# A transformer block in fp32: first MLP weights split during the attention and kept in DRAM

## The chip, the cores and the metric

The kernel runs on one core of a Trainium2 chip. The metric is device time in microseconds (us) of one execution. PE is TensorE, PEld its weight loads, DVE is VectorE, ACT is ScalarE, POOL is GpSimd, and SP is SyncE, which here issues every DMA.

## The reference

One block on 2048 tokens of width 576, fp32, with 32 query heads that share one key and value head of 18 columns:

```python
mod = (silu(c) @ w_mod).reshape(1, 6, 1, 576)
sa, ca, ga, sb, cb, gb = (mod[:, i] for i in range(6))
h = layernorm(x) * (1 + ca) + sa
q = h @ wq                       # 32 heads of 18
k, v = h @ wk, h @ wv            # one head
p = softmax(q k^T * 18 ** -0.5)  # 2048 x 2048 per head
x = x + ga * ((p v) @ wo)
h = layernorm(x) * (1 + cb) + sb
y = layernorm(h)
x = x + gb * (gelu(y @ w1 + b1) @ w2 + b2)   # hidden width 4608
```

## The kernel before

All matrix products on PE use fp32r operands. A value is kept as a high part, which is the value rounded to fp32r, and a low part, which is the value less the high part; a product is then three products (high-high, high-low, low-high). Making such a pair costs a copy and a subtraction, and where these are made is a large share of what ACT, DVE and POOL do.

The order of the work is written out by hand. Every engine runs its instructions in the order in which the program states them, and so does SP with its DMAs: an instruction that waits holds back all that stand behind it on its engine.

**Stage 1** makes the projections and the first layer norm. **Stage 2** is the attention. It goes through 32 "quads" (n = 0 to 31: four blocks of 512 tokens, by eight groups of four heads). A quad has 16 slots (kc = 0 to 15, 128 keys each). In a slot PE makes scores (`st_mm`, L792), ACT takes their exponentials (L794), and PE multiplies by V (`pv_mm`, L781); beside that PE makes the scores again in the other orientation for the NEXT quad (L313, L802), and DVE takes the row maxima (L814, L812). At the end of each slot `between(n, kc)` adds the rest:

- At kc = 12 and 13 (`smax_fin1`, `smax_fin2`) the maxima of the next quad are put together, transposed, split by POOL into `ms` (L355, L356) and sent by four DMAs into the query tile `qst` of the next quad (L360).
- `post_quad` normalizes the finished quad, one piece a slot: DVE transposes (L616), POOL multiplies by the reciprocal into `T` (L620), DVE transposes back (L622), ACT and POOL split it (L629, L630), and four DMAs put `os` into the attention's result (L634).
- At kc = 1 `load_q` clears and loads a query tile (two POOL memsets, L130; six DMAs, L309).
- In odd slots the queue `fill` takes one step. It holds the `wo` product of a finished block (L593, eight steps) and then, for blocks 0 and 1, the MLP's norm (`ln2_block`, four `ln2_tile` of 128 tokens each).
- In odd slots from n = 3 on, the queue `prep` takes one step. Before the change it makes the split pairs of the second MLP weights: load, scale by BC (L715), copy (L718), subtract (L720), write to the DRAM tensor `w2scr` (L721).

`ln2_tile` is two layer norms in a row on one tile. POOL does the multiplications by BC and the addition of `b2` always; the two passes that subtract the mean and scale (L534, L548) run on POOL where `fine` is true, for blocks 0 and 1, and on DVE for blocks 2 and 3, which are done inside the MLP. PE then transposes the tile in two steps.

**Stage 3** starts with the `wo` product of the last block (tiles t = 0 to 3, two halves each) and then runs the MLP in 36 rounds (v = 0 to 35): 18 groups g of 256 hidden columns, for the first 1024 tokens and again for the last. A round makes seven products with a Strassen-like scheme (`product`, L944): operands A11, S2, S3, A12, S1, A22, S4 of the first weights, the S ones being sums or differences of blocks. It then runs the GELU (L956 to L964) and, one round later, the second product (`fc2`, L979), whose result DVE adds to `XT` (L983). Before the change the seven operands of round v + 1 are made anew inside round v: `load_w1` loads the raw weights (L657), `w1_sum`, `w1_part` and `w1_tails` form sums and pairs on POOL (L664, L667, L683, L702 to L706) and ACT (L662). `first_split` does this for round 0 in the last quad. `load_w2` reads the pairs of the second weights from `w2scr`. `op_pieces` forms the other side's operands from the transposed norm, in rounds 0 and 17. The norm tiles of blocks 2 and 3 are taken step by step by `more` in rounds 1 to 16; a step that ends in "T" marks a PE transpose, which only some places take.

The pool `px`, which holds the working tiles of `prep` and `post_quad`, has one buffer for each name, unless a tile says otherwise:

```python
    pxp = tc.tile_pool(name="px", bufs=1, reuse_waits="tile")
```

Of the kernel before, what the change touches and what calls it, by code (L numbers as in the profile page):

```python
# [15 lines left out]
NB = 4  # L16
TB = S // NB
NT = TB // 128
KD = 5
# [13 lines left out]
def block_kernel(ctx: ExitStack, tc, x, wqkv, wo, w1, b1, w2, b2, c, wmod, ident_in, out):  # L33
# [31 lines left out]

    w2scr = dr.tile([NG, 128, 2, 2, D], F32, name="w2scr")
# [429 lines left out]
    def late_weights():  # L496

        gab = pb.tile([128, D], F32, name="gab")
        for j, dst, scl in ((2, gab, 1.0), (5, BC[:, 2, :], 0.5)):
            wm = load_mod(j)  # L500
            for _ in range(4):
                yield
            yield from mod_bcast(wm, px.tile([128, 640], F32, name="Z2"), dst, 0.0, scl)
        wor = bigw(D)
        sy.dma_start(wor, wo)
        wos = pw.tile([128, 2, KD, D], F32R, name="wos", tag="wA", padded_shape=[128, 2, KD, WQC])
        WOH, WOL = WO["h"], WO["l"] = wos[:, 0], wos[:, 1]
        for k in range(KD + 2):
            if k < KD:
                po.tensor_mul(wor[:, k, :], wor[:, k, :], gab)  # L510
            if 0 <= k - 1 < KD:
                ac.activation(WOH[:, k - 1, :], wor[:, k - 1, :], AF.Copy)
            if k >= 2:
                po.tensor_tensor(WOL[:, k - 2, :], wor[:, k - 2, :], WOH[:, k - 2, :].bitcast(F32), op=ALU.subtract)
            yield

    def ln2_tile(tb, t):
# [6 lines left out]
        fine = tb < 2  # L524
# [31 lines left out]
        yield None if fine else "T"  # L556
# [50 lines left out]
    def post_quad(n, PV):  # L607
# [13 lines left out]
        yield  # L621
        ve.transpose(O, T.rearrange("p a b -> p (a b)"))  # L622
# [18 lines left out]
    W1 = {}  # L641

    def w1_tile():
        W1["r"] = per.tile([128, 40, 128], F32R, name="w1a", tag="big", bufs=3)

    def w1_rooms():
        while prep:
            step(prep)
        W1["a"] = px.tile([128, KD, 2, 128], F32, name="w1r")
        t = px.tile([128, 3, 128], F32, name="w1s")  # L650
        W1["s"], W1["d"] = t[:, :2], t[:, 2]

    def w1_raw(f, h):
        return W1["a"][:, 2 * h:2 * h + 2, f, :]

    def load_w1(i):
        sy.dma_start(W1["a"].rearrange("p k f c -> p k (f c)"), w1[i])  # L657

    def w1_hi(a, n, src, e=ac):
        o = W1["r"][:, a:a + n]  # L660
        if e is ac:
            ac.activation(o, src, AF.Copy)  # L662
        else:
            e.tensor_copy(o, src)  # L664

    def w1_lo(a, n, src, e):
        e.tensor_tensor(W1["r"][:, 17 + a:17 + a + n], src, W1["r"][:, a:a + n].bitcast(F32), op=ALU.subtract)  # L667

    def w1_part(a, lo, e=po):

        n, src = (4, W1["a"][:, :KD - 1, 0, :]) if a == 0 else (2, w1_raw(1, 1))
        if lo:
            w1_lo(a, n, src, e)
        else:
            w1_hi(a, n, src)

    SUMS = {4: "S2", 6: "S3", 10: "S1", 12: "S4"}

    def w1_sum(a, e=po):

        o = W1["s"]
        def op(x, y, how):
            e.tensor_tensor(o, x, y, op=how)  # L683
        if SUMS[a] == "S3":
            op(w1_raw(0, 0), w1_raw(1, 0), ALU.subtract)
        elif SUMS[a] == "S4":
            op(w1_raw(0, 1), W1["r"][:, 4:6].bitcast(F32), ALU.subtract)
            op(o, W1["r"][:, 21:23].bitcast(F32), ALU.subtract)
        else:
            op(w1_raw(1, 0), w1_raw(1, 1), ALU.add)  # L690
            if SUMS[a] == "S2":
                op(o, w1_raw(0, 0), ALU.subtract)
        w1_hi(a, 2, o, e if e is po else ac)
        w1_lo(a, 2, o, e)

    def w1_tails(lo, e=po):

        t, d = W1["a"][:, KD - 1], W1["d"]
        if not lo:
            w1_hi(14, 2, t)  # L700
            return
        e.tensor_tensor(d, t[:, 0], t[:, 1], op=ALU.subtract)  # L702
        e.tensor_copy(W1["r"][:, 16], d)
        for o, i in ((slice(14, 16), t), (16, d)):
            h = W1["r"][64:, o]
            e.tensor_tensor(h, i[64:], h.bitcast(F32), op=ALU.subtract)  # L706

    def w2_parts():

        for g in range(NG):  # L710
            for f in range(2):
                o = px.tile([128, D], F32, name="w2o", tag="w1s")
                sy.dma_start(o, w2[g, :, f, :])
                yield
                po.tensor_tensor(o, o, BC[:, 2, :], op=ALU.mult)  # L715
                yield
                hl = px.tile([128, 2, D], F32R, name="w2p", tag="w1r")
                po.tensor_copy(hl[:, 0], o)  # L718
                yield
                po.tensor_tensor(hl[:, 1], o, hl[:, 0].bitcast(F32), op=ALU.subtract)  # L720
                sy.dma_start(w2scr[g, :, :, f, :], hl.bitcast(F32))  # L721
                yield

    prep = deque([w2_parts()])

    def first_split():
        w1_tile()
        w1_rooms()
        load_w1(0)
        for _ in range(3):  # L730
            yield
        w1_sum(4, ve)
        w1_part(0, False)
        yield
        w1_part(0, True)
        w1_sum(6, ve)
        yield
        w1_part(8, False)
        w1_sum(10, ve)
        w1_tails(False)  # L740
        yield
        w1_part(8, True)
        w1_sum(12, ve)
        yield
        w1_tails(True)
        yield
# [69 lines left out]
    def between(n, kc):  # L816
# [10 lines left out]
        if kc == 0 and n == NQT - 1:  # L827
            fill.append(first_split())
# [4 lines left out]
        if kc % 2:  # L833
            step(fill)
            if n > 2:
                step(prep)

# [34 lines left out]
    def op_pieces(R, e2):  # L872
# [23 lines left out]
    wop = {(t, h2): (psC if t == 3 and h2 else psM if t < 2 and t + h2 < 2 else psB)()  # L896
           for t in range(NT) for h2 in range(2)}
    for t in range(NT):
        for h2 in range(2):
            wo_mm(NB - 1, t, h2, wop[t, h2], 0, KD - 1)  # L900
# [8 lines left out]
    pwp.__exit__(None, None, None)  # L909
    px = ctx.enter_context(tc.tile_pool(name="mx", bufs=1, reuse_waits="tile"))  # L910
    tl = ctx.enter_context(tc.tile_pool(name="tl", bufs=1, side="right", reuse_waits="tile"))
    TL.append(tl.tile([128, 4, TB], F32R, name="opt"))
    form("+t0 -t0")
    for t in range(NT):
        for h2 in range(2):
            wo_mm(NB - 1, t, h2, wop[t, h2], KD - 1, KD)
            wo_add(NB - 1, t, h2, wop[t, h2])
    form("+t1 =T4 =T1 +T1 -t1 -T1")
    open_ps("3", 4)
    w1_rooms()  # L920
    B2["b"] = load_b2()
    load_w1(1)
    GT = big()
    U = px.tile([128, 2, TB], F32, name="u")
    W2 = [px.tile([128, 2, D], F32R, name="w2s", bufs=3) for _ in range(3)]
    W2.append(W1["r"][:, 31:40].rearrange("p a b -> p (a b)").rearrange("p (f c) -> p f c", f=2))
    W2 = W2[:2], W2[2:]
# [6 lines left out]
    def product(o, w, b, first=True, tail=None):  # L934

        h, l = W1["r"][:, w:w + 2], W1["r"][:, 17 + w:19 + w]
# [3 lines left out]
        if tail:  # L940
            wt = W1["r"][:, 14 + tail[0]]
            terms += [(wt, TL[0][:, tail[1]]), (wt, TL[0][:, 2 + tail[1]])]
# [6 lines left out]
    def gelu(v, f, b, p):  # L949
# [13 lines left out]
        ac.activation(GT[:, 2 * u], h, AF.Copy)  # L963
        po.tensor_tensor(GT[:, 2 * u + 1], h, GT[:, 2 * u].bitcast(F32), op=ALU.subtract)  # L964

    def fc2(v):
        h2, l2 = W2[v % 2]
        for bt in range(2 * NT):
# [3 lines left out]
            for nn in range(2):  # L972
                cs = slice(288 * nn, 288 * (nn + 1))
                terms = []
                for f in range(2):
                    gh, gl = (GT[:, 2 * G[v, b, f] + l, ts_] for l in range(2))
# [27 lines left out]
    for v in range(NV):  # L1004
        nx = v + 1 < NV
# [5 lines left out]
        def more(half="", first="", room=False):  # L1011

            if v in (0, NG - 1, NG):
                form(first if v == 0 else half if v == NG - 1 else "-T1 -B22 -t1" if first == "+T4" else "")
# [5 lines left out]
        def wt(f, *a):  # L1020
            if nx:
                f(*a)

        load_w2(v)
        ba = psB()
        product(ba, 0, 0)
# [4 lines left out]
        product(bb, 4, 6)  # L1031
# [6 lines left out]
        product(bc, 6, 10)  # L1038
        ve.tensor_tensor(U[:, 1], bc, U[:, 0], op=ALU.add)
        wt(w1_sum, 4)  # L1040
        more("-T2 =T3", "+B22", True)
        t_()
        if v == 1:
            t_()
        product(ba, 2, 2, False, (0, 0))
        gens.append(gelu(v, 0, 0, ba))
        g_()
        wt(w1_part, 0, False)
        more("+T3 +B21", "-B22", True)
        t_()  # L1050
        g_()
        wt(w1_sum, 6)
        wt(w1_part, 0, True)
        bd = psB()
        product(bd, 10, 8, True, (1, 1))
# [5 lines left out]
        more("-T3 -B21 =T4")  # L1061
        t_()
        g_()
        wt(w1_sum, 10)
        product(bc, 8, 12, False, (1, 0))
# [4 lines left out]
        wt(w1_part, 8, False)  # L1070
        more("=T1 +T4 +t0")
# [3 lines left out]
        wt(w1_part, 8, True)  # L1075
        product(bd, 12, 4, False, (2, 1))
# [4 lines left out]
        wt(w1_tails, False)  # L1081
        t_()
        wt(w1_sum, 12)
        wt(w1_tails, True)
        more("-T4 -t0 +T1 +B22 +t1")
        drain(f2)
        f2 = fc2(v)
        if v + 2 < NV:
            load_w1((v + 2) % NG)
# [43 lines left out]
```

## Time and profile before

| | |
|---|---|
| median of 3 runs | 2371.99 us (2367.28 to 2372.89) |
| the profiled execution | 2367.2 us, its span 2365.4 us |
| granted PE clock | 0.993 |
| busy | PE 2310.6, DVE 1822.6, ACT 1693.2, POOL 1157.7 us |
| DMA | 155.30 MB, 66 GB/s on average |

The profile shows one execution. Rows of a group give busy time, the mean of one instruction in ns, and the idle time of the engine before them with what ended it. "x <- y" in a row of waits means that x waited for y. "SPq" is SP's queue, and its durations are the issue of the DMA, not the transfer. The attention lasts from about 139 us to 1433 us, the MLP from there to the end; a quad is some 38 to 51 us, a round some 24 to 32.

### The profile page before, as it was taken

What the parts mean: (1) busy time and instruction counts of PE and PEld (TensorE: products, weight loads), DVE (VectorE), ACT (ScalarE), POOL (GpSimd) and SP (SyncE); (2) the same over time, 40 slices, a digit from 0 to 9 for tenths busy, and PEclk for the clock granted to TensorE, in tenths of its full rate; (3) what the DMA queues carried; (4) which work ended last, traced back from release to release, by engine and by line L of the source; (5) the groups of instructions that cost most, each with busy time, mean ns of one, the idle gap of its engine ahead of it and who ended that gap; (6) DMA issues with size and microseconds to landing.
All of it is one profiled execution on the core that took longest, in us unless ns stands there. A gap on an engine that the chain in (4) does not pass through costs nothing.

```text
span 2365.4 us, 44038 instructions
## 1 busy us (share of the span) xinstructions
PE 2310.6 (98%) x16586; PEld 1456.1 (62%) x16586; DVE 1822.6 (77%) x3242; ACT 1693.2 (72%) x3264; POOL 1157.7 (49%) x1402
## 2 busy tenths in 40 slices
PE   8999999999999999999999999999999999999999
PEld 5643444454344443444544436889898989999998
DVE  6589999979999889999799955666676665565655
ACT  5569999979999889999799996444444544444443
POOL 6501332324552235431101013888888787777774
PEclk9999999999999999999999999999999999999999
DMA  6412122211222112200000001211211221212112
GB/s 219 141 60 72 39 67 64 75 55 50 66 68 78 45 54 70 62 19 22 9 19 22 19 23 37 94 63 63 94 63 63 94 103 63 94 63 93 64 69 86
DMA packets 63206, 155.30 MB, mean 66 GB/s; under 512 B 7835, under 2 KB 11547, under 8 KB 62993
## 3 DMA queue, kind: packets, MB, share of 16 engines
q1 hardware_dynamic: 62993, 152.48, 19.5%
q8 instruction: 131, 2.15, 0.4%
q14 instruction: 82, 0.67, 0.1%
HBM read 108.17 MB, written 35.39 MB: 61 GB/s over the span
## 4 chain that ended last, share of the span: by engine, by line
PE 89%; DVE 3%; ACT 3%; POOL 3%; issue 1%; DMA 1%; SPq 0%; POOLq 0%; DVEq 0%; ACTq 0%
PE psC L781 21%; PE psA L979 19%; PE psB L944 17%; PE psB L792 11%; PE psM L313 10%; PE psB L802 4%; PE psB L593 2%; PE psB L242 2%; ACT P L794 2%; DVE mx L814 1%; PE psB L150 1%; PE psA L313 1%; PE psB L197 1%; ACT O L612 1%; DMA bigw<-in_wmod 0%
## 5 line engine op out<-in xcount | busy, mean ns | idle before, releaser
L794 ACT ACTIVATE P<-psB 128x512 f32<-128x512 f32 x2048 | 1051.4, 623 | 5.1 <-PE psB L792 3.9
L814 DVE TENSOR_REDUCE mx<-psM 128x1 f32<-128x512 f32 x1476 | 944.3, 683 | 57.5 <-PE psM L313 33.0
L781 PE MATMUL psC<-P,V 128*32 128x256 f32 (+1 forms) x6056 | 599.5, 467 | 13.1 <-ACT O L612 13.1
L313 PE MATMUL psM<-KS,qst 64*128 64x512 f32 x1722 | 595.8, 432 | 5.0 <-DVE mx L814 5.0
L792 PE MATMUL psB<-qst,KS 64*128 64x512 f32 x2048 | 600.0, 435 | 0.3 <-DMA qst<-ms 0.3
L979 PE MATMUL psA<-w2s,big 128*128 128x288 f32 x2880 | 498.1, 297 | 8.5 <-DVE XT L983 8.5
L979 PEld LDWEIGHTS psA<-w2s,big 128*128 128x128 f32 x2880 | 434.6, 190 | 23.7 <-DVE XT L983 9.7
L792 PEld LDWEIGHTS psB<-qst,KS 64*128 64x128 f32 x2048 | 306.2, 185 | 166.9 <-issue 72.5
L944 PE MATMUL psB<-ops,w1a 128*128 128x512 f32 x1512 | 390.8, 398 | 4.6 <-POOL w1a L667 2.1
L313 PEld LDWEIGHTS psM<-KS,qst 64*128 64x128 f32 x1722 | 285.1, 185 | 125.5 <-DVE mx L812 84.4
L983 DVE TENSOR_TENSOR XT<-psA,XT 128x576 f32<-128x576 f32 x288 | 216.7, 753 | 180.0 <-PE psA L979 179.7
L944 PEld LDWEIGHTS psB<-ops,w1a 128*128 128x128 f32 x1512 | 273.7, 189 | 56.0 <-POOL w1a L667 2.6
L781 PEld LDWEIGHTS psC<-P,V 128*32 128x32 f32 x6056 | 119.7, 108 | 232.8 <-issue 209.1
L963 ACT ACTIVATE big<-gx 128x512 fp32r<-128x512 f32 x144 | 91.1, 633 | 234.8 <-DVE gx L962 234.8
L964 POOL TENSOR_TENSOR big<-gx,big 128x512 fp32r<-128x512 f32 x144 | 187.3, 1301 | 129.6 <-ACT big L963 89.6
L805 ACT ACTIVATE xc<-psB 128x512 f32<-128x512 f32 x246 | 148.1, 602 | 91.4 <-PE psM L313 76.1
L355 POOL CAST ms<-mf 16x128 fp32r<-16x128 f32 x32 | 9.0, 280 | 408.8 <-ACT mf L354 408.8
L956 ACT ACTIVATE gx<-psB,b1t 128x512 f32<-128x512 f32 x144 | 97.3, 675 | 105.8 <-PE psB L944 97.3
L979 PE MATMUL psA<-w1a,big 128*128 128x288 f32 x576 | 169.7, 295 | 0.0
L812 DVE CUSTOM_DVE_ANT_0 xc<-psM,xc 128x512 f32<-128x512 f32 x246 | 167.4, 680 | 0.0
L960 ACT ACTIVATE psB<-gs 128x512 f32<-128x512 f32 x144 | 86.5, 601 | 94.3 <-DVE gs L959 94.3
L959 DVE SCALAR_TENSOR_TENSOR gs<-psB,gx 128x512 f32<-128x512 f32 x144 | 98.8, 686 | 70.2 <-ACT psB L957 70.1
(168 smaller groups left out, 2626.2 us busy)
## 6 DMA issues: line engine op xcount, KB each, us to landing
w2s<-w2scr SPq DMA_DIRECT2D x54, 576.0 KB
w1r<-in_w SPq DMA_DIRECT2D x36, 640.0 KB
w2scr<-w2p SPq DMA_DIRECT2D x36, 576.0 KB
qst<-qscr SPq DMA_DIRECT2D x192, 72.0 KB
w2o<-in_w SPq DMA_DIRECT2D x36, 288.0 KB
w1a<-w2scr SPq DMA_DIRECT2D x18, 576.0 KB
qscr<-qs SPq DMA_DIRECT2D x16, 504.0 KB
big<-os SPq DMA_DIRECT2D x112, 72.0 KB
```

The source lines that it names most:

```text
L313: pe.matmul(o, QST[n][64 * g:64 * g + 64, p, 128 * qt:128 * (qt + 1)], KS[64 * g:64 * g + 64, 512 * kb:512 * (kb + 1)], start=True, stop=True)
L781: pe.matmul(PVt[n][32 * j:32 * (j + 1), cs], V[:, kc, :], t[:, j, cs], start=(kc == 0 and h0 == 0), stop=(kc == 15), skip_group_check=True)
L792: pe.matmul(t, KS[64 * g:64 * g + 64, 128 * kc:128 * (kc + 1)], QST[n][64 * g:64 * g + 64, i, :], start=True, stop=True)
L794: ac.activation(P[n, kc][:, 2 * i + g, :], t, AF.Exp, scale=SCALE)
L805: ac.activation(XC[-1], t, AF.Relu)
L812: ve.tensor_tensor_reduce(c, t, c, 1.0, -3.0e38, ALU.add, ALU.max, o)
L814: ve.tensor_reduce(o, t, axis=AX.X, op=ALU.max)
L944: pe.matmul(o, x, y, start=(first and i == 0), stop=(i == len(terms) - 1), skip_group_check=True)
L959: ve.scalar_tensor_tensor(s, p, 1.0 / GA3, h, op0=ALU.add, op1=ALU.mult)
L964: po.tensor_tensor(GT[:, 2 * u + 1], h, GT[:, 2 * u].bitcast(F32), op=ALU.subtract)
L979: pe.matmul(p[:, nn, :288], x, y, start=(q == 0), stop=(q == len(terms) - 1))
L983: ve.tensor_tensor(Xv, p[:, :, :288], Xv, op=ALU.add)
```

## The change

The seven operands of each group of first weights, as split pairs, are made once, in the attention, by POOL, and written to a new DRAM tensor `w1scr` (18 groups of 128 x 31 x 128). The generator `weight_parts` takes the place of `w2_parts` in the queue `prep` and makes both weights of a group in 15 steps. `prep` is stepped in every slot from n = 3 on except slots 10 to 13, in place of odd slots alone. In the MLP each operand is loaded from `w1scr` in place, right after the product that read the one before it; the code that made them there goes, and so does `first_split`. `ln2_tile` is `fine` for all blocks. In `post_quad` there is one more slot between POOL's T and DVE's transpose. The last block's `wo` product uses the MLP's PSUM layout: three tiles ahead of it, the fourth in pieces within round 0.

```diff
+    w1scr = dr.tile([NG, 128, 31, 128], F32, name="w1scr")
...
-        gab = pb.tile([128, D], F32, name="gab")
+        gab = px.tile([128, D], F32, name="gab", tag="r2")
...
-        fine = tb < 2
+        fine = True
...
-        yield None if fine else "T"
+        yield "T"
...
         e.tensor_tensor(T, T, R[:, :, None].to_broadcast([128, 16, 32]), op=ALU.mult)
         yield
+        if e is po:
+            yield
         ve.transpose(O, T.rearrange("p a b -> p (a b)"))
...
+    OPS = ("A11", "S2", "A12", "S3", "S1", "A22", "S4")
+    def load_w1(i, what):
+        for w in what.split():
+            a = 4 * OPS.index(w) if w in OPS else 28
+            b = min(a + 4, 31)
+            sy.dma_start(W1["r"][:, a:b].bitcast(F32), w1scr[i, :, a:b])
+
+    def weight_parts():
+        def two(o, n, src, lo=None):
+            po.tensor_copy(o[:, :n], src)
+            po.tensor_tensor(o[:, n:2 * n], src, o[:, :n].bitcast(F32), op=ALU.subtract)
         for g in range(NG):
+            raw = px.tile([128, KD - 1, 2, 128], F32, name="r1")
+            sy.dma_start(raw.rearrange("p k f c -> p k (f c)"), w1[g][:, :KD - 1])
+            yield
+            yield
+            def blk(f, h):
+                return raw[:, 2 * h:2 * h + 2, f, :]
+            def part(w, src):
+                o = px.tile([128, 4, 128], F32R, name="r2")
+                two(o, 2, src)
+                a = 4 * OPS.index(w)
+                sy.dma_start(w1scr[g, :, a:a + 4], o.bitcast(F32))
+            sm = px.tile([128, 2, 128], F32, name="r3")
+            def add(x, y, how=ALU.subtract):
+                po.tensor_tensor(sm, x, y, op=how)
+            part("A11", blk(0, 0))
+            yield
+            part("A12", blk(0, 1))
+            yield
+            part("A22", blk(1, 1))
+            add(blk(1, 0), blk(1, 1), ALU.add)
+            yield
+            part("S1", sm)
+            add(sm, blk(0, 0))
+            yield
+            part("S2", sm)
+            add(blk(0, 1), sm)
+            yield
+            part("S4", sm)
+            add(blk(0, 0), blk(1, 0))
+            yield
+            part("S3", sm)
+            raw = px.tile([128, 2, 128], F32, name="r1")
+            sy.dma_start(raw.rearrange("p f c -> p (f c)"), w1[g][:, KD - 1])
+            yield
+            yield
+            d = px.tile([128, 128], F32, name="r3")
+            o = px.tile([128, 3, 128], F32R, name="r2")
+            po.tensor_tensor(d, raw[:, 0], raw[:, 1], op=ALU.subtract)
+            for x, y in ((o[:, :2], raw), (o[:, 2], d)):
+                po.tensor_copy(x, y)
+                po.tensor_tensor(x[64:], y[64:], x[64:].bitcast(F32), op=ALU.subtract)
+            sy.dma_start(w1scr[g, :, 28:31], o.bitcast(F32))
+            raw = px.tile([128, 2, D], F32, name="r1")
+            sy.dma_start(raw, w2[g])
+            yield
+            yield
+            po.tensor_tensor(raw, raw, BC[:, 2:3, :].to_broadcast([128, 2, D]), op=ALU.mult)
+            yield
             for f in range(2):
+                for nn in range(2):
+                    cs = slice(288 * nn, 288 * (nn + 1))
+                    o = px.tile([128, 2, 288], F32R, name="r2")
+                    two(o, 1, raw[:, f:f + 1, cs])
+                    sy.dma_start(w2scr[g, :, :, f, cs], o.bitcast(F32))
                 yield
+    prep = deque([weight_parts()])
...
-        if kc == 0 and n == NQT - 1:
-            fill.append(first_split())
...
             step(fill)
-            if n > 2:
+        if n > 2 and (kc < 10 or kc > 13):
+            step(prep)
+        if kc == 8 and n == NQT - 1:
+            while prep:
                 step(prep)
+            W1["r"] = per.tile([128, 40, 128], F32R, name="w1a", tag="big", bufs=3)
+            load_w1(0, " ".join(OPS) + " tails")
...
-                    ve.tensor_tensor(o, x, y, op=ALU.subtract)
+                    (e2 if w == "=T1" else ve).tensor_tensor(o, x, y, op=ALU.subtract)
...
+    open_ps("3", 4)
+    wop = {}
+    def wo_tile(t, k0, k1):
+        if t not in wop:
+            p = psA() if t != 2 else None
+            wop[t] = [psB()[:, :288] if t == 2 else p[:, h2, :288] for h2 in range(2)], p
         for h2 in range(2):
+            wo_mm(NB - 1, t, h2, wop[t][0][h2], k0, k1)
+        if k1 == KD:
+            o, p = wop[t]
+            if p is None:
+                for h2 in range(2):
+                    wo_add(NB - 1, t, h2, o[h2])
+            else:
+                Xv = XT[:, NT * (NB - 1) + t, :].rearrange("p (a b) -> p a b", a=2)
+                ve.tensor_tensor(Xv, p[:, :, :288], Xv, op=ALU.add)
+    for t in range(3):
+        wo_tile(t, 0, KD - 1)
...
+    rest = deque((3, k, k + 1) for k in range(KD))
...
+            if v == 0 and rest:
+                for _ in range(2):
+                    if rest:
+                        wo_tile(*rest.popleft())
+                if not rest:
+                    wo_end()
+        def w_(w):
+            if v + 1 < NV:
+                load_w1((v + 1) % NG, w)
+        if v:
+            load_w2(v)
         ba = psB()
-        product(ba, 0, 0)
+        product(ba, "A11", 0)
+        w_("A11")
...
-        wt(w1_sum, 4)
...
-        wt(w1_part, 0, False)
...
-            load_w1((v + 2) % NG)
```

More of the change, by code (lines that the diff above doesn't have):

```diff
@@ L552, in ln2_tile @@
         po.tensor_tensor(X, X, B2["b"], op=ALU.add)
-        yield None if fine else "T"
+        yield "T"
         yr = YR[tb // 2][:, KD * (tb % 2):KD * (tb % 2 + 1)]
         transpose_tile(Z, yr, t, 0, 4, ac)
-        yield None if fine else "T"
+        yield "T"
         transpose_tile(Z, yr, t, 4, 5, ve)
@@ L641, in block_kernel @@
     W1 = {}
[L643 to L708, printed above, removed]
-        for g in range(NG):
-            for f in range(2):
-                o = px.tile([128, D], F32, name="w2o", tag="w1s")
-                sy.dma_start(o, w2[g, :, f, :])
-                yield
[L715 to L746, printed above, removed]
+    OPS = ("A11", "S2", "A12", "S3", "S1", "A22", "S4")
@@ L908, in block_kernel, with wo_end @@
     pxp.__exit__(None, None, None)
-    pwp.__exit__(None, None, None)
-    px = ctx.enter_context(tc.tile_pool(name="mx", bufs=1, reuse_waits="tile"))
     tl = ctx.enter_context(tc.tile_pool(name="tl", bufs=1, side="right", reuse_waits="tile"))
     TL.append(tl.tile([128, 4, TB], F32R, name="opt"))
+    px = ctx.enter_context(tc.tile_pool(name="mx", bufs=1, side="right", reuse_waits="tile"))
     form("+t0 -t0")
[L914 to L917, printed above, removed]
+    for t in range(3):
+        wo_tile(t, KD - 1, KD)
     form("+t1 =T4 =T1 +T1 -t1 -T1")
-    open_ps("3", 4)
-    w1_rooms()
+    rest = deque((3, k, k + 1) for k in range(KD))
     B2["b"] = load_b2()
-    load_w1(1)
-    GT = big()
     U = px.tile([128, 2, TB], F32, name="u")
-    W2 = [px.tile([128, 2, D], F32R, name="w2s", bufs=3) for _ in range(3)]
-    W2.append(W1["r"][:, 31:40].rearrange("p a b -> p (a b)").rearrange("p (f c) -> p f c", f=2))
-    W2 = W2[:2], W2[2:]
+    W2, GT = [], []
+    def wo_end():
+        pwp.__exit__(None, None, None)
+        mw = ctx.enter_context(tc.tile_pool(name="mw", bufs=1, reuse_waits="tile"))
+        a = [mw.tile([128, 2, D], F32R, name="w2s", bufs=3) for _ in range(3)]
+        a.append(W1["r"][:, 31:40].rearrange("p a b -> p (a b)").rearrange("p (f c) -> p f c", f=2))
+        W2.extend((a[:2], a[2:]))
+        GT.append(big())
+        load_w2(0)
     NV = 2 * NG
@@ L934, in product @@
     def product(o, w, b, first=True, tail=None):
-        h, l = W1["r"][:, w:w + 2], W1["r"][:, 17 + w:19 + w]
+        w = 4 * OPS.index(w)
+        h, l = W1["r"][:, w:w + 2], W1["r"][:, w + 2:w + 4]
         terms = []
@@ L975, in fc2 @@
                 for f in range(2):
-                    gh, gl = (GT[:, 2 * G[v, b, f] + l, ts_] for l in range(2))
+                    gh, gl = (GT[0][:, 2 * G[v, b, f] + l, ts_] for l in range(2))
                     terms += [(gh, h2[:, f, cs]), (gh, l2[:, f, cs]), (gl, h2[:, f, cs])]
@@ L1004, in block_kernel @@
     for v in range(NV):
-        nx = v + 1 < NV
         if v == NG - 1:
@@ L1013, in more @@
             if v in (0, NG - 1, NG):
-                form(first if v == 0 else half if v == NG - 1 else "-T1 -B22 -t1" if first == "+T4" else "")
+                form(first if v == 0 else half if v == NG - 1 else {"+T4": "-T4 +T1 -B22", "-T4": "-T1 -t1"}.get(first, ""))
             elif v < NG and fill and (room or mark[0] != "T"):
@@ L1030, in block_kernel @@
         bb = psB()
-        product(bb, 4, 6)
+        product(bb, "S2", 6)
+        w_("S2")
         ve.tensor_tensor(U[:, 0], bb, U[:, 0], op=ALU.add)
@@ L1037, in block_kernel @@
         bc = psB()
-        product(bc, 6, 10)
+        product(bc, "S3", 10)
+        w_("S3")
         ve.tensor_tensor(U[:, 1], bc, U[:, 0], op=ALU.add)
-        wt(w1_sum, 4)
         more("-T2 =T3", "+B22", True)
+        if v != 1:
+            t_()
+        product(ba, "A12", 2, False, (0, 0))
+        w_("A12")
+        gens.append(gelu(v, 0, 0, ba))
+        g_()
+        more("+T3 +B21", "-B22", True)
         t_()
@@ L1044, in block_kernel @@
             t_()
-        product(ba, 2, 2, False, (0, 0))
-        gens.append(gelu(v, 0, 0, ba))
-        g_()
-        wt(w1_part, 0, False)
[L1049 to L1053, printed above, removed]
+        g_()
         bd = psB()
-        product(bd, 10, 8, True, (1, 1))
+        product(bd, "S1", 8, True, (1, 1))
+        w_("S1")
         be = psB()
@@ L1060, in block_kernel @@
         g_()
-        more("-T3 -B21 =T4")
+        more("-T3 -B21")
         t_()
-        g_()
-        wt(w1_sum, 10)
-        product(bc, 8, 12, False, (1, 0))
+        if v == 1:
+            t_()
+        g_()
+        product(bc, "A22", 12, False, (1, 0))
+        w_("A22")
         ve.tensor_tensor(bc, bc, U[:, 0], op=ALU.add)
@@ L1069, in block_kernel @@
         g_()
-        wt(w1_part, 8, False)
-        more("=T1 +T4 +t0")
+        more("=T4 +t0")
         t_()
@@ L1074, in block_kernel @@
         t_()
-        wt(w1_part, 8, True)
-        product(bd, 12, 4, False, (2, 1))
+        product(bd, "S4", 4, False, (2, 1))
+        w_("S4 tails")
         ve.tensor_tensor(bd, bd, U[:, 0], op=ALU.add)
@@ L1080, in block_kernel @@
         g_()
-        wt(w1_tails, False)
         t_()
-        wt(w1_sum, 12)
-        wt(w1_tails, True)
-        more("-T4 -t0 +T1 +B22 +t1")
+        more("=T1 +T4 -t0 +B22 +t1")
         drain(f2)
         f2 = fc2(v)
-        if v + 2 < NV:
-            load_w1((v + 2) % NG)
     while gens:
```

14 lines of the change are left out of this document (3 added, 11 removed).

## The prediction

> **What bounds the kernel now.** I read the page first (which engine is full, and where), then windows cut at the quads of the attention and at the rounds of the MLP, then the groups of instructions with their idle time, and last GpSimd's and SyncE's own rows in time.
>
> ```profile
> PE 2310.6 (98%) x16586; PEld 1456.1 (62%) x16586; DVE 1822.6 (77%) x3242; ACT 1693.2 (72%) x3264; POOL 1157.7 (49%) x1402
> POOL 6501332324552235431101013888888787777774
> ...
> 300.00:338.40 38.40, 37.94 (x323) 15.41 (x320) 36.42 (x70) 37.71 (x76) 11.84 (x13) 1.00 0.22 65
> 667.40:707.30 39.90, 39.18 (x326) 16.40 (x325) 38.26 (x77) 37.69 (x76) 21.84 (x22) 1.00 0.21 61
> 2104.30:2128.70 24.40, 24.40 (x148) 22.12 (x147) 14.31 (x21) 11.30 (x21) 17.96 (x25) 1.00 0.20 77
> ```
>
> In the windows the columns are the stretch, its length, then busy time of PE, PE's loads, DVE, ACT and POOL, the granted clock, DMA share and GB/s. A plain quad of the attention (300 to 338) has three full engines: PE 37.9, ACT 37.7 and DVE 36.4 of 38.4 us. What any of them waits for is lost. POOL has 26 us free there, and 18 us in a quad with a norm tile (667 to 707). A steady MLP round is PE alone, 24.4 of 24.4; POOL's 18.0 and ACT's 11.3 are covered. So POOL's work goes from a stage where it is covered by PE to one where nothing has slack, if POOL keeps another engine waiting.
>
> Does POOL have deadlines in the attention? Three rows of its timeline, and two that show what a late one costs:
>
> ```profile
> 308.01 1.05 POOL L620 TENSOR_TENSOR T<-T,R 128x512 f32<-128x512 f32 x1 [7.48 <-DVE R L619]
> 333.61 0.28 POOL L355 CAST ms<-mf 16x128 fp32r<-16x128 f32 x1 [9.32 <-ACT mf L354]
> ...
> L792 PE MATMUL psB<-qst,KS 64*128 64x512 f32 x2048 | 600.0, 435 | 0.3 <-DMA qst<-ms 0.3
> ...
> 597.74 0.71 DVE L622 STREAM_TRANSPOSE O<-T 128x512 f32<-128x512 f32 x1 [1.62 <-POOL T L620]
> 595.00:599.00 4.00, 2.67 (x24) 1.01 (x16) 2.38 (x5) 3.72 (x8) 3.92 (x4) 1.00 0.25 63
> 586.40:628.40 42.00, 40.04 (x328) 16.36 (x326) 37.84 (x76) 38.28 (x76) 24.99 (x25) 0.96 0.21 63
> 599.00:603.00 4.00, 3.56 (x20) 1.42 (x24) 3.49 (x8) 2.37 (x5) 1.36 (x2) 0.60 0.00 0
> ```
>
> Each quad, POOL now sits idle 7.5 us before T and 9.3 us before ms, so both run the moment they can. ms feeds the next quad's scores: PE waited for that DMA once, 0.3 us, so it lands just in time and a later ms is a later quad. At 597.74 POOL came 1.6 us late with T, PE was busy for 2.7 of those 4 us, the clock fell to 0.60 in the next 4, and that quad took 42.0 instead of 38.4.
>
> **The change, part by part.** New is a chain through one buffer: tile r2 has one copy, so each POOL copy into it waits until the DMA of the piece before has landed in DRAM. The prices:
>
> ```profile
> L664 POOL CAST w1a<-w1s 128x256 fp32r<-128x256 f32 x140 | 57.6, 411 | 9.1
> L667 POOL TENSOR_TENSOR w1a<-w1s,w1a 128x256 fp32r<-128x256 f32 x140 | 104.0, 743 | 11.2
> L718 POOL CAST w2p<-w2o 128x576 fp32r<-128x576 f32 x36 | 23.7, 658 | 0.0
> L715 POOL TENSOR_TENSOR w2o<-w2o,BC 128x576 f32<-128x576 f32 x36 | 51.2, 1422 | 76.2 <-DMA w2o<-in_w 76.2
> L702 POOL TENSOR_TENSOR w1s<-w1r 128x128 f32<-128x128 f32 x36 | 16.7, 465 | 0.0
> L703 POOL CAST w1a<-w1s 128x128 fp32r<-128x128 f32 x36 | 10.5, 292 | 2.3
> L706 POOL TENSOR_TENSOR w1a<-w1r,w1a 64x256 fp32r<-64x256 f32 x36 | 26.6, 738 | 2.9
> ...
> 2361.51 0.76 DVE L983 TENSOR_TENSOR XT<-psA,XT 128x576 f32<-128x576 f32 x1 [0.82 <-PE psA L979]
> 2351.64 10.99 SPq L985 DMA_DIRECT2D out<-XT  x8
> SPq L1129 <- DMA out<-XT: 1.7, 1, 1.7
> ...
> 1939.40 0.34 SPq L657 DMA_DIRECT2D w1r<-in_w  x1
> 1943.55 0.74 POOL L683 TENSOR_TENSOR w1s<-w1r 128x256 f32<-128x256 f32 x1 [2.02 <-DMA w1r<-in_w]
> ```
>
> The last output write (288 KB) gives the round trip: its source is ready at 2362.27, SP has issued it at 2362.63, and waits 1.7 more: 2.06 us. I take that for a 256 KB piece, and 2.3 for those whose issue is of the 0.6 us kind (L721, below). Reads: 640 KB took 4.15 us (1939.40 to 1943.55); I take 3.7 for 512 KB and 4.0 for 576 KB.
>
> One weight group, in POOL's order: load of raw w1 3.7; seven parts of 0.41 + 0.74 + 2.06 = 3.21, together 22.5 (the four sums of 0.74 lie inside the waits); tails 0.47 + 0.41 + 0.74 + 0.29 + about 0.46 = 2.4; load of w2 4.0; its product, twice 1.42 = 2.8; four pieces of w2 at 288 columns, about 0.43 + 0.81 each, 5.0, with three waits of 2.3, 6.9. Sum 47.3, with some 28 gaps of 0.06 between instructions 49. Busy are 21 of it; the rest is waiting, and POOL is in order. A group has 15 steps and a quad 12, so **a quad asks 39.2 us of this chain against the 38.4 that it lasts**. The step-free slots 10 to 13 are only where it catches up. It takes 270 / 12 = 22.5 quads, from n = 3 to 25.
>
> What else a quad asks of POOL is 11.84 less the two old w2 pieces (3.5 each): 4.9. And SP puts its other DMAs ahead of a pending write:
>
> ```profile
> 277.10 1.43 POOL L720 TENSOR_TENSOR w2p<-w2o,w2p 128x576 fp32r<-128x576 f32 x1
> 276.44 3.36 SPq L634 DMA_DIRECT2D big<-os  x4
> 279.91 0.61 SPq L721 DMA_DIRECT2D w2scr<-w2p  x1
> 333.92 3.16 SPq L360 DMA_DIRECT2D qst<-ms  x4
> 337.86 2.70 SPq L309 DMA_DIRECT2D qst<-qscr  x6
> 587.01 0.23 POOL L144 TENSOR_SCALAR rs<-mv 128x1 f32<-128x1 f32 x1 [3.94 <-DVE mv L143]
> 587.32 0.57 POOL L145 TENSOR_TENSOR rs<-rs,nhalf 128x1 f32<-128x1 f32 x1
> ```
>
> At 278.5 POOL was done, and the write went out at 279.9, behind four os DMAs. Per quad these blocks are 3.4 + 3.2 + 2.7 = 9.3. If all 14.2 us hide in the chain's waits, a plain quad costs +0.8; if none, +15. Most of it does meet a wait; I take 3.7 as left over, so +4.5. Beside a norm tile POOL has 9.5 us more a quad (8 of 9 steps of 10.7: twice rs, 0.80; twice the pass at L534, 2.31, quoted below; three of 1.42; a small copy). Half hidden, that makes 47.7 against 39.9, and DVE, which waits for POOL's Z in its own order with its max reductions queued behind, adds about one: +9 (ends 0 and +23). T has one slot of 2.4 us more than before, which covers a lag of that size. Quads: 9 with norm tiles (74 steps by 8), about 7 plain ones after the first; the five with wo are 42 to 51 us long and absorb it. **Attention: 7 x 4.5 + 9 x 9 = +112.**
>
> The Trainium skill, "DMA: Bandwidth & Descriptors", section on the anatomy of one DMA, puts a transfer at about 2.0 us plus its bytes at 436 GB/s, 2.6 us for a part; the 2.06 row is shorter, and the row decides. By the page the ten round trips of a group would add 5.4 us, a quad 4.3, sixteen quads 69, and the time would be 2537.
>
> The MLP loses the w1 sums on POOL, the casts on ACT, and the w1r load. In steady rounds that is worth nothing (PE covers it). Where PE waits:
>
> ```profile
> 1450.00:1475.00 25.00, 20.40 (x89) 15.51 (x88) 17.82 (x27) 13.77 (x23) 16.69 (x19) 0.97 0.28 87
> 1574.00:1603.10 29.10, 26.74 (x153) 23.97 (x152) 18.82 (x29) 11.88 (x22) 23.78 (x32) 0.94 0.17 64
> 1701.80:1728.10 26.30, 25.12 (x152) 22.45 (x152) 17.56 (x29) 12.03 (x23) 23.66 (x32) 1.00 0.20 71
> 1777.40:1803.80 26.40, 25.24 (x153) 22.57 (x152) 16.31 (x25) 12.07 (x23) 23.89 (x29) 1.00 0.19 71
> 1876.90:1908.60 31.70, 26.37 (x148) 23.80 (x147) 23.75 (x28) 16.29 (x27) 23.64 (x26) 0.89 0.16 58
> 1881.48 3.95 DMA w1r<-in_w
> 1895.22 2.31 POOL ops L892
> L534 POOL TENSOR_SCALAR Z<-XT,mv,rs 128x576 f32<-128x576 f32 x8 | 18.5, 2308 | 0.2
> L534 DVE TENSOR_SCALAR Z<-XT,mv,rs 128x576 f32<-128x576 f32 x8 | 7.8, 973 | 3.2 <-POOL rs L145 3.2
> ```
>
> The round at 1877 is 7.3 over 24.4: the w1r load and the POOL work after it go, the ops pieces on POOL stay (2.3 each) and are late next: -5. The round at 1702: -1.4. Those at 1574 and 1777 (6.7 over) wait for a norm tile; two passes of it become 1.3 us slower each (2.31 against 0.97) on a POOL that has lost the w1 work: -3. The start (1450 to 1475 has 4.6 us without PE): the fourth wo tile, 30 products moved into round 0, fills it: -4. Sum -13.4, ends -4 and -20. The reload of w1 (31 x 64 KB a round, with w2 3.1 MB in 24.4 us, 130 GB/s) costs nothing: SP waits at each piece for PE's last read, and the pieces and w2 queued behind it are due a round later; without that cover a piece costs its 2 us round trip. The first load, eight DMAs at slot 8 of the last quad, and the extra DRAM traffic are covered the same way. The last wo sums in pairs of banks and the first split gone from the last quad are worth nothing: DVE has 24.4 - 14.3 free in a round.
>
> **Sum:** the profiled execution took 2367.2 (span 2365.4); 2367.2 + 112 - 13.4 = 2466. The median shown is 4.8 above the profiled one, so 2468.
>
> **The rivals.** (a) *The waits hide*: POOL runs ahead of PE in idle time, ms and T stay on time, and only the MLP's gain is left: 2354. For it: POOL idles 26 us a plain quad. Against it: 39.2 against 38.4, with nothing else counted. It decides from a round trip of 1.3 us down: 39.2 - 8 x 0.76 + 4.9 = 38.0. (b) *Only norm quads suffer*: plain quads fit, the nine lose about 4: +36 - 13 = 2390. (c) *Loss and gain meet*: about 1.5 in each norm quad, within 7 us of before. (d) *The clock doubles it*: at 599 a gap of PE was followed by 0.60 for 4 us, 1.6 us lost; in 16 quads +26, 2494. The Trainium skill, "TensorE: Matmul & The Clock Gate", part 1, has the clock halve after an idle window of about 3.4 us; the 0.60 row agrees.
>
> **How the numbers follow.** Likeliest, both kinds of quad late: 0.50, its own range 2410 to 2540. (d) 0.08, (b) 0.16, (c) 0.06, (a) 0.20. 0.3% (7 us) is what a measurement of this kernel can tell from no change. Slower 0.74, same 0.06, faster 0.20. The range takes in (a) and stops short of "nothing hides": 2352 to 2540.
>
> **What would show it.** Right: POOL's r2 copies waiting for w1scr writes, some 250 us or more in all; PE waiting for qst<-ms far beyond 0.3; DVE waiting for T and Z; plain quads near 43 and norm quads near 48; the MLP some 13 us shorter, rounds still 24.4. Wrong: POOL still idle ahead of ms in each quad, with quads of 38.4 (then (a)); or a round trip well under 2 us.

## The result, and the profile after

The changed kernel takes 2505.5 us (median, 2503.3 to 2507.5) against 2370.8 before: a ratio of 1.057, 95% interval 1.055 to 1.059, so 135 us slower. The forecast was 2468, slower, in a range of 2352 to 2540.

The page of the changed kernel, the lines on busy time and on POOL in 40 slices:

```profile
PE 2367.2 (95%) x16586; PEld 1464.7 (58%) x16586; DVE 1799.5 (72%) x3204; ACT 1656.1 (66%) x3152; POOL 989.1 (39%) x1189
POOL 6503444446565444566543110144344342222121
```

POOL does less in total (989 us, before 1158), since the first weights' operands are made once, not twice. It does more in slices 5 to 20, where PE, ACT and DVE were full. The profiled execution, with the same 16586 products, is 139 us longer.

Windows of the changed kernel, the columns as before: two plain quads with the preparation, one beside a norm tile, one after the preparation has ended, and a steady round.

```profile
299.40:349.00 49.60, 41.81 (x324) 16.46 (x321) 38.22 (x72) 38.83 (x77) 22.87 (x34) 0.93 0.28 94
349.00:392.90 43.90, 40.81 (x321) 16.27 (x321) 36.59 (x69) 37.97 (x75) 19.91 (x29) 0.93 0.31 101
634.10:686.70 52.60, 41.57 (x326) 16.89 (x326) 37.71 (x74) 38.46 (x76) 32.36 (x42) 0.93 0.27 90
1366.30:1404.70 38.40, 37.95 (x323) 15.58 (x324) 36.52 (x70) 37.71 (x76) 4.95 (x6) 1.00 0.08 21
2243.40:2267.80 24.40, 24.40 (x148) 22.14 (x147) 14.34 (x22) 10.04 (x17) 5.22 (x5) 1.00 0.40 133
```

The quad is 38.4 again as soon as the preparation is over (1366). In the first of these quads no engine is full, and POOL is busy for 22.9 of 49.6 us, less than half. That is not an engine without room, it is an engine that waits. What it waits for, from the waits of the changed kernel (first three lines), and who then waits for POOL:

```profile
POOL r L657 <- DMA w1scr<-r: 145.3, 88, 4.3
POOL r L657 <- DMA w2scr<-r: 140.6, 52, 5.1
POOL r L657 <- DMA r<-in_w: 52.9, 16, 5.7
...
PE psB L769 <- DMA qst<-ms: 53.7, 15, 8.2
DVE bst L139 <- POOL Z L537: 59.4, 15, 9.0
DVE O L625 <- POOL T L621: 16.9, 6, 3.7
PE psB L151 <- POOL Z L549: 15.8, 5, 6.4
```

(L657 is the copy into r2, L673 and L720 the writes, L769 the scores, L356 ms.) POOL waits 286 us for writes out of r2. The loads into r1, which has one buffer too, cost it another 137 us (52.9 at L657, 42.8 at L713 and 41.3 at L704). The three deadlines named ahead are all missed: PE waits 53.7 us for ms (0.3 before), and in the attention DVE waits 26.5 for Z (0.4 before) and 16.9 for T (5.0 before). The other 32.9 of the 59.4 us at Z lie in the MLP, at the eight norm tiles whose passes now run on POOL. A fourth wait was not named ahead: PE itself waits 15.8 us for the second pass of Z (L549), which it transposes; before, it didn't.

POOL's and SP's own rows in the first of these quads:

```profile
305.06 2.66 POOL L713 TENSOR_TENSOR r<-r,BC 128x1152 f32<-128x1152 f32 x1 [4.63 <-DMA r<-in_w]
310.29 0.81 POOL L658 TENSOR_TENSOR r<-r,r 128x288 fp32r<-128x288 f32 x1
314.06 0.42 POOL L657 CAST r<-r 128x288 fp32r<-128x288 f32 x1 [2.97 <-DMA w2scr<-r]
318.56 0.80 POOL L658 TENSOR_TENSOR r<-r,r 128x288 fp32r<-128x288 f32 x1
321.97 0.42 POOL L657 CAST r<-r 128x288 fp32r<-128x288 f32 x1 [2.61 <-DMA w2scr<-r]
328.69 0.40 POOL L657 CAST r<-r 128x256 fp32r<-128x256 f32 x1 [4.19 <-DMA r<-in_w]
329.17 0.74 POOL L658 TENSOR_TENSOR r<-r,r 128x256 fp32r<-128x256 f32 x1
332.08 0.40 POOL L657 CAST r<-r 128x256 fp32r<-128x256 f32 x1 [2.17 <-DMA w1scr<-r]
344.75 0.28 POOL L356 CAST ms<-mf 16x128 fp32r<-16x128 f32 x1
...
323.86 0.61 SPq L662 DMA_DIRECT2D r<-in_w  x1
345.05 2.84 SPq L361 DMA_DIRECT2D qst<-ms  x4
```

A part ends at 329.91 (329.17 and 0.74) and the next copy starts at 332.08: 2.17 us of round trip for 1.14 of work. ms (344.75) has no wait in its row, where before it had POOL idle 9.3 us ahead of it: it comes when POOL gets there. SP issues its DMAs as soon as it is there (345.05).

Quad by quad (from one ms to the next), the six plain ones from n = 4 on grew by 41 us, the ten beside norm tiles by 102, the six with wo by 15, and those from n = 26 on, after the preparation, by nothing. The last block's wo product starts at 1592.0, before at 1435.9: **attention +156**. From there to the end are 912.4 us, before 929.6: **MLP -17**.

### The profile page after: what moved, and what is told of

Same layout as the page of the kernel before. It is cut to its first block, busy times and chain, and to the rows that moved or that the text cites. A ratio compares the mean times of both kernels' runs of the same rounds, so it can differ in the third digit from the quotient of the medians.

```text
span 2504.4 us, 44373 instructions
## 1 busy us (share of the span) xinstructions
PE 2367.2 (95%) x16586; PEld 1464.7 (58%) x16586; DVE 1799.5 (72%) x3204; ACT 1656.1 (66%) x3152; POOL 989.1 (39%) x1189
## 4 chain that ended last, share of the span: by engine, by line
PE 62%; POOL 14%; DMA 14%; issue 3%; ACT 3%; DVE 2%; SPq 2%; POOLq 0%; ACTq 0%; DVEq 0%
PE psA L978 18%; PE psB L943 16%; PE psC L758 10%; PE psB L769 5%; DMA w1scr<-r 5%; PE psM L314 4%; DMA r<-in_w 4%; POOL r L658 4%; DMA w2scr<-r 4%; POOL r L657 2%; PE psB L243 2%; PE psB L594 2%; PE psB L779 2%; ACT P L771 2%; POOL r L713 1%
## 5 line engine op out<-in xcount | busy, mean ns | idle before, releaser
L769 PE MATMUL psB<-qst,KS 64*128 64x512 f32 x2048 | 626.7, 454 | 54.4 <-DMA qst<-ms 53.7
L314 PE MATMUL psM<-KS,qst 64*128 64x512 f32 x1722 | 622.0, 446 | 34.1 <-DVE mx L791 33.7
L758 PE MATMUL psC<-P,V 128*32 128x256 f32 (+1 forms) x6056 | 619.4, 482 | 8.0 <-ACT O L613 7.8
L769 PEld LDWEIGHTS psB<-qst,KS 64*128 64x128 f32 x2048 | 312.6, 193 | 231.7 <-issue 135.4
L314 PEld LDWEIGHTS psM<-KS,qst 64*128 64x128 f32 x1722 | 298.0, 193 | 170.6 <-DVE mx L789 84.3
L657 POOL CAST r<-r 128x256 fp32r<-128x256 f32 (+1 forms) x198 | 80.4, 406 | 340.0 <-DMA w1scr<-r 145.3
L658 POOL TENSOR_TENSOR r<-r,r 128x256 fp32r<-128x256 f32 (+1 forms) x198 | 150.0, 758 | 15.9
```

Source lines behind the costliest of these rows:

```text
L314: pe.matmul(o, QST[n][64 * g:64 * g + 64, p, 128 * qt:128 * (qt + 1)], KS[64 * g:64 * g + 64, 512 * kb:512 * (kb + 1)], start=True, stop=True)
L658: po.tensor_tensor(o[:, n:2 * n], src, o[:, :n].bitcast(F32), op=ALU.subtract)
L758: pe.matmul(PVt[n][32 * j:32 * (j + 1), cs], V[:, kc, :], t[:, j, cs], start=(kc == 0 and h0 == 0), stop=(kc == 15), skip_group_check=True)
L769: pe.matmul(t, KS[64 * g:64 * g + 64, 128 * kc:128 * (kc + 1)], QST[n][64 * g:64 * g + 64, i, :], start=True, stop=True)
```

## The experiments

Theory A: POOL, which works in order, waits for each write out of the single r2 to land, its chain of a group's 15 steps takes longer than the quads give it, and ms, T and Z come late. Rival B: POOL's added work itself does it, by its length or at the SBUF. Rival C: the added DMAs do it, on SP's queue or in the DMA engines. The first five experiments were measured once each; the differences read from them are some 20 us or more, where the median of before moves by 4 us from chip to chip.

**const_src.** The writes take a constant tile as their source:

```diff
-                sy.dma_start(w1scr[g, :, a:a + 4], o.bitcast(F32))
+                sy.dma_start(w1scr[g, :, a:a + 4], BC[:, 0, :512].rearrange("p (a b) -> p a b", a=4))
```

and the same for the tails and for w2.

> All POOL work of the weight preparation stays, and all its DMAs in number and size; only their source is a constant tile instead of r2, so w1scr and w2scr get columns of BC and the values are not the weights. POOL's copies into r2 then wait for no write. Theory A (the wait of POOL, in order, for the landing of each write out of the single r2): the attention loses some 20 us instead of 156, mostly beside the norm tiles and at the three loads of a group, and the time is 2360 to 2390. Rival B (POOL's 17 us of extra work a quad, or its sharing of SBUF with DVE, is what is late): no change, about 2505. Rival C (the DMA traffic, or SP's queue, delays the query rows): about 2505 too.

Measured 2369.6 (before, on the same chip: 2368.2). The attention ends at 1455.4, 137 us earlier than in the changed kernel. A quad of it, and PE's wait for ms:

```profile
299.40:338.00 38.60, 38.15 (x327) 15.65 (x323) 36.65 (x70) 37.95 (x76) 22.65 (x34) 1.00 0.36 120
PE psB L769 <- DMA qst<-ms: 1.3, 3, 0.8
```

POOL is as busy as in the 49.6 us quad (22.65 against 22.87 us) and the DMA moves more per second (120 GB/s against 94), and the quad is 38.6. B falls as the main cause, and so does the traffic of C. SP's queue is not tested by this run alone, since its writes no longer wait for POOL here either (551 us at L673 and L720 in the changed kernel). For ms the changed kernel's own rows settle it: in every quad its DMAs start to go out within 0.6 us of its being made, so it is late at POOL and not at SP. And slow10, below, keeps 566 us of these waits of SP and is 58 us faster.

**dma_only.** POOL's work of the preparation is left out as well.

> As const_src, and POOL's copies, subtractions, sums and products of the preparation are left out too (weights again not the real ones). Only the loads and writes are left in the attention. Theory A and B: quads as before the change, the attention ends near 1436, and the time shows the MLP's gain alone, 2345 to 2358. Rival C: the attention is still long, 2450 or more.

Measured 2347.6, 21 us below before; the attention ends at 1433.6, 2 earlier than before, and the MLP takes 912.2, 17 less. So the DMAs alone cost the attention nothing. A quad of it:

```profile
300.00:338.40 38.40, 37.54 (x319) 15.02 (x311) 36.52 (x71) 37.61 (x75) 4.95 (x6) 1.00 0.35 121
```

The difference to const_src, 22 us, is what POOL's work and the waits for loads cost by themselves; its quads 11, 12, 19 and 20, beside norm tiles, are 4 to 5 us longer than in dma_only. In const_src POOL still waits 82 us for loads.

**two_r2.** A second buffer, made room for:

```diff
-                o = px.tile([128, 4, 128], F32R, name="r2")
+                o = px.tile([128, 4, 128], F32R, name="r2", bufs=2)
...
-                for nn in range(2):
-                    cs = slice(288 * nn, 288 * (nn + 1))
+                for nn in range(3):
+                    cs = slice(192 * nn, 192 * (nn + 1))
```

> r2 has two buffers (to fit, w2 pieces are 192 columns instead of 288 and gab lies in r1). POOL's work and the DMAs stay, a few instructions more. Theory A: a write has one more piece's time to land, so most of the 2.2 us wait goes: the attention loses 45 to 70 us instead of 156, the time 2395 to 2420. Rival B: 2505 or a few us more. Rival C: 2505 or more, for there are 36 more writes.

Measured 2394.4, 111 us less than the changed kernel and just below the range expected. The tails and the w2 pieces get the second buffer too. Its waits on r2's writes fall to a third:

```profile
POOL r L657 <- DMA w2scr<-r: 67.4, 43, 3.9
POOL r L657 <- DMA w1scr<-r: 17.5, 15, 3.6
PE psB L769 <- DMA qst<-ms: 8.1, 5, 3.0
```

Plain quads are 38.3 to 39.8; those beside norm tiles still 42 to 47.

**slow10.** Ten steps a quad:

```diff
-        if n > 2 and (kc < 10 or kc > 13):
+        if n > 2 and (kc < 8 or kc > 13):
```

> Ten steps of the preparation in a quad instead of twelve (none in slots 8 to 13), so it takes 27 quads instead of 22.5. Theory A: a plain quad asks 34 us of the chain instead of 41 and nearly fits, norm quads still lose: the attention loses 80 to 110 us, the time 2430 to 2460. Rival B (loss per piece of work, wherever it stands): the same total, about 2505. Rival C: the same, about 2505.

Measured 2447.2. The same work and the same number of round trips, spread over more quads, cost 58 us less. What counts is what a quad is asked for.

**ms_off_pool.** One of the deadlines is taken from POOL:

```diff
-        po.tensor_copy(ms[:, 0], mf)
-        po.tensor_tensor(ms[:, 1], mf, ms[:, 0].bitcast(F32), op=ALU.subtract)
+        ac.activation(ms[:, 0], p[:16, :128], AF.Copy, scale=-1.0)
+        ve.tensor_tensor(ms[:, 1], mf, ms[:, 0].bitcast(F32), op=ALU.subtract)
```

> The changed kernel, with the two small ms operations of each quad on ACT and DVE instead of POOL, so that POOL's lag can't delay the next quad's query rows (54 us of PE's waits in the changed kernel). Theory A, in its throughput form (POOL's chain asks more than a quad lasts, and the quad stretches until it fits, whichever deadline stops it): the loss moves to T and the norm's Z, and the time is 2480 to 2510. Rival (each late deadline is a loss of its own): the 54 us go, about 2450.

Measured 2483.3, 22 us less. Its waits, and two of SP's own queue:

```profile
DVE bst L139 <- POOL Z L537: 61.1, 16, 8.5
PE psB L769 <- DMA qst<-ms: 30.9, 11, 7.8
DVE O L625 <- POOL T L621: 19.9, 8, 4.0
...
SPq L673 <- POOL r L658: 333.2, 108, 8.9
SPq L720 <- POOL r L658: 242.3, 65, 11.2
...
660.66 0.28 DVE L357 TENSOR_TENSOR ms<-mf,ms 16x128 fp32r<-16x128 f32 x1 [0.25 <-ACT ms L356]
660.20 8.38 SPq L720 DMA_DIRECT2D w2scr<-r  x3
669.35 2.87 SPq L361 DMA_DIRECT2D qst<-ms  x4
```

Not all of the 54 us went: PE still waits 30.9 for the same DMA. T (19.9) is as late as in the changed kernel, and so is Z (28.2 of the 61.1 lie in the attention, 26.5 there). SP issues in order too: its writes at L673 and L720 wait for POOL, and the ms DMAs stand behind them. In the last three rows ms is made at 660.9, three writes of w2 pieces stand ahead of it, and its DMAs go out at 669.4, 8.4 us late. The throughput form holds more than the additive one, though the ms path did carry 22 of the 135.

**two_r2_slots** and **slots_norm_dve.** Fewer steps beside norm tiles; then, in addition, the MLP's norm passes back on DVE:

```diff
-        if n > 2 and (kc < 10 or kc > 13):
+        if n > 2 and (kc % 2 == 0 and kc not in (10, 12) if 9 < n < 15 or 17 < n < 23 else kc < 10 or kc > 13):
...
-        e = po if fine else ve
+        e = po if tb < 2 else ve
```

> two_r2, and in the quads beside norm tiles (n = 10 to 14 and 18 to 22) only six steps of the preparation, in the even slots 14, 0, 2, 4, 6, 8, where no norm step is; twelve elsewhere. In two_r2 the plain quads were already 38.3 to 39.8 and the norm quads 42 to 47 against 39 to 42 before. Theory A: the norm quads come down to 39 to 43, the attention loses 5 to 18 us in all, the MLP keeps 912, and the time is 2352 to 2368, 0.1 to 0.8% below before. Rival (POOL's extra work costs the same wherever it stands): 2394 as in two_r2.

> two_r2_slots with the two mean-and-scale passes of the MLP's norm tiles (blocks 2 and 3) back on DVE. My step had the move to POOL worth some 3 us as part of the rounds that wait for a norm tile; if POOL's 1.3 us a pass hide in its idle time, the times are within 3 us of two_r2_slots; if the move is what the MLP gained, this is 5 to 10 us slower; if POOL's longer passes are what is late next, 3 to 6 us faster.

Measured 2374.2 and 2370.0, against 2368.2 of before: ratios 1.0022 (1.0012 to 1.0032) and 1.0004 (0.9994 to 1.0015). The first missed its bracket by 6: some norm quads were still long (13: 47.5, 20: 45.0). The second is 4 faster than the first, the third of the cases expected. It takes 909.2 for its MLP against 912.4: POOL's longer passes were late at the start. The chain of the changed kernel there:

```profile
1632.46 2.31 POOL Z L535
1634.85 1.41 POOL Z L536
1636.32 1.40 POOL Z L537
1638.12 0.75 DVE XT L982
```

DVE waits for Z with the sum into XT behind it, and PE waits for that: 4.3 us in all, 1.9 with the passes on DVE. The rest of the two kernels' difference lies in the attention, which that edit does not touch: 3.7 us between the two traces.

**slots3, slots1, slots4.** On slots_norm_dve, the eight full norm quads get three, one or four steps, the others twelve (slots1: the wo quads 14):

```diff
+        if n > 2 and (kc in (0, 4, 8) if n in (10, 11, 12, 13, 18, 19, 20, 21) else kc < 10 or kc > 13):
```

> slots_norm_dve with the preparation moved further away from the norm tiles: three steps (slots 0, 4, 8) in the eight quads that are norm tiles throughout (n = 10 to 13, 18 to 21), twelve in all others. Theory A (what is left of the loss, quads of 42 to 48 beside norm tiles, is Z late behind a step that waits for a load or a write): those quads come near 39 to 42 as in dma_only, and the time is 2350 to 2364. Rival (the loss follows POOL's work, not its place): 2370, as slots_norm_dve.

> The same with one step (slot 0) in those eight quads, and two more (slots 10, 11) in the longer quads with the wo product (n = 8, 9, 16, 17, 24, 25). Theory A: at or below slots3, 2346 to 2362; if the steps at slots 10 and 11 make ms late, the wo quads grow by 2 to 5 each and it is above slots3. Rival: 2370.

> slots3 with a fourth step (slot 14) in the eight norm quads, so that the preparation ends in quad 30 and the first w1 load isn't held up at the start of the MLP (in slots3 the chain there shows the last w2scr write, the load's issues and 4.7 us of w1 load one behind the other). Theory A: the start gains 4 to 8, the eight norm quads lose at most 0.5 each: 2345 to 2354. If slot 14's step makes Z late, 2354 to 2362.

slots3 measured 2354.0, a ratio of 0.993 (0.992 to 0.994): 0.7% below before, and the fastest kernel here that makes the real weights, with wo_early. slots1 is 2370.4 (0.9999, 0.9991 to 1.0008) and slots4 2368.4 (0.9990, 0.9981 to 0.9999), both above what was expected. slots3's only wait of PE for ms, then slots4's in one window of 60 us:

```profile
PE psB L769 <- DMA qst<-ms: 0.2, 1, 0.2
...
POOL r L657 <- DMA w2scr<-r: 7.4, 2, 3.9
PE psB L769 <- DMA qst<-ms: 5.8, 1, 5.8
```

In slots4 the norm quads (39 to 44) lose 5 us more than in slots3, and quads 29 and 30, at 44.4 and 43.2 where slots3 has 38.6 and 37.7, lose 11: other steps of the 15 now stand ahead of ms there. In slots1, outside the norm quads, those that grew most are 23, 26, 27 and 30 (41 to 42), which have twelve steps as in slots3; the wo quads with 14 grew by 0 to 2. So which steps fall ahead of a deadline matters at this size, and the number of steps alone does not say it. That this phase is the cause was not tested by itself.

**wo_early.** In slots3, the fourth wo tile ahead of round 0 again:

```diff
-    rest = deque((3, k, k + 1) for k in range(KD))
+    wo_tile(3, 0, KD)
+    rest = deque()
```

> slots3 with the fourth wo tile multiplied ahead of round 0, as the other three, instead of in pieces within it; the rest of the bank layout stays. My step had the move worth 4 us (it fills PE's idle time in round 0): then 2356 to 2360. Rival: round 0 is held by other waits (the operands, the first w1 load), and the 30 products only change places: within 2 us of slots3.

Measured 2353.8: no difference, as the rival had it. Round 0 is 4.0 us shorter (11.7 against 15.7) and the stretch ahead of it 4.0 longer (17.3 against 13.3). The split of the last tile is worth nothing here. In slots3 the start also waits for the first w1 load, which is issued 8 us ahead of the wo product (17 in the changed kernel), so for the changed kernel this is likely and not shown.

## Why the prediction was right, and where it was off

- **What bounds the kernel, and the chain through r2:** right. The waits stand where they were put (286 us at r2, forecast some 250 or more), const_src takes them away and 136 us with them, and two_r2 takes most.
- **The round trip, 2.06 us from the last output write:** 2.17 for a part. For the w2 pieces I took 2.3; the rows above have 2.97 and 2.61, and the median of the 43 pieces with nothing between them and the next copy is 2.69. The load of raw w1 is 4.8 from issue to first reader (3.7), that of w2 4.2 (4.0), and the tails start 2.7 after the last part's end, where the sum had the write's 2.06. That is some 4 us more a group. Two w2 products are 56 to 58 us apart in plain quads, where I had 49 for a group, so twelve steps take 45 to 46; the plain quads are 43 to 50, on the mean 45.2. The other 4 us of a group are not divided up here: POOL's T, os, ms and memsets stand in the same order.
- **Plain quads +4.5:** the term was too small, 6.9 each (41 us in six). The 3.7 us in it for what doesn't hide was chosen between 0 and 14 without a row to say so. **Norm quads +9:** 10.2 (102 us in ten, I counted nine); that term was near.
- **"The five with wo absorb it": half right.** There are six. The three of 51 us (n = 9, 17, 25) do absorb it, with 1 us more in all; the three of 42 us (n = 8, 16, 24) don't and grew by 14. This fits a chain that asks 45 us a quad.
- **Attention +112, measured +156; MLP -13.4, measured -17.2.** The round at 1877 fell from 31.6 to 24.4 (-7, forecast -5), those that waited for a norm tile by 4.7, 1.4 and 2.0 or so (forecast 4.4 together), the start by 2 (forecast 4). The reason given for the start is in doubt too: in wo_early the moved products bring nothing. Steady rounds are 24.4 as before, with 133 GB/s of DMA in all, most of it w1.
- **The sum itself:** 2466 and 4.8 make 2471, not 2468, which is small against the 37 us by which the forecast missed.
- **Rival (a), the waits hide:** it needed a round trip under 1.3 us, and the part's is 2.17. **(b):** in two_r2, where plain quads do fit, this is the picture, 2394 where I had put 2390.
- **(d), the clock:** the granted clock is 0.87 to 0.97 in the plain and norm quads of the preparation. In the clock records it stands at 0.50 for 154 us in all, 37 before. Half of the 117 us more is 59, and PE's busy time is 57 us more for the same products. That is the most that the slower clock adds to PE's own work; as the quads there last as long as POOL's chain, how much of the 135 it does add can't be told from these runs. The prediction has the 0.60 row agree with an idle window of 3.4 us. Cut finer, the clock there is 0.50 for 3.4 us from 599.8 on, so the half and its length agree, but PE's gap ahead of it lasts 1.8 us (597.67 to 599.44), not 3.4.
- The page "DMA: Bandwidth & Descriptors" of the Trainium skill gives its formula for the path of DMAs that GpSimd issues; by it, as an estimate, a 256 KB part takes 2.6 us and a piece of 288 KB 2.7. Here SP issues them, and measured were 2.17 and 2.69, so the formula fits the pieces and is 0.4 too long for the parts; the one row I took fits the parts and is too short for the pieces. The sum worked out by it, 2537 (2531 if three of the ten round trips stand at the 2.3 that the sum has), lay 32 above the measured time, mine 37 below. That it came as near is luck: most of what it adds is time that the parts don't take.

## What to carry to other kernels

Free time of an in-order engine is not room for work that goes out through one buffer: cost each piece at its work plus the write's round trip, compare the sum with the stretch it must fit in, and count who needs that engine on time. Move such work away from the stretches where the engine has short deadlines, give it a second buffer first, and then time the placement, since a few steps more or fewer decide between 2354 and 2370 here.

## What the runs showed of the hardware that was not expected

A 256 KB write whose 2 KB per partition go to one place had its source free 2.17 us after it was ready; a 288 KB one, two pieces of 1152 bytes per partition, 2.61 to 2.97 in the rows above, of which 0.23 is the longer issue on SP (0.56 against 0.33, medians). Twice the DMA traffic in the attention (121 GB/s in a quad of dma_only, 65 before) cost PE, ACT and DVE nothing: both quads last 38.4 us. A single gap of 1.8 us in PE's products was followed by half the clock for 3.4 us.
